# Fillers, early sums, highs, lows and the plan of an attention and expert kernel

## The chip, the cores and the metric

One core of one Trainium2 chip runs the whole program. The metric is the device time of one execution in microseconds; three executions of the kernel before took 981.32, 982.22 and 983.5 us, median 982.22.

## What is computed

The reference is an attention with a threshold, followed by four experts whose outputs are added with weights:

```python
scores = q @ k.T / sqrt(64)                    # q, k, v: 4 batches, 8 heads, 576 x 64
scores = where(scores >= max(scores) - tau, scores, -1e9)
attn = exp(scores - max(scores)); attn /= sum(attn)
x = (attn @ v)                                 # as 2304 rows of 512
p = domain_probs / sum(domain_probs)
for e in range(4):                             # w1: 512 x 1024, w2: 1024 x 512
    out += p[:, e:e + 1] * (relu(x @ w1[e]) @ w2[e])
```

## The kernel before, in words

**Numbers in two halves.** Everything is float32 in memory. Most products on PE are made from pairs of float16: a "high" is the value times a power of two, rounded to float16, and a "low" is what the rounding left; high x high, high x low and low x high are added in PSUM. The powers of two come from sums of squares: an engine squares a tensor and sums along the row (`squares`, L510), PE adds over partitions with a matrix of ones (`total`, L530), and five small DVE operations make the scale (`pow2`, L539). ACT or another engine then writes the high with that scale, and DVE the low with one operation on two inputs. The first batch's attention is done in float32 instead, and needs no highs and lows of q, k and v.

**Items and groups.** The attention is cut into 80 items (`item`, L1046): a pair of heads and a block of 128 queries, or the last 64 of each head. PE writes scores into tile S, which has one buffer of three banks (L1004, L1010); DVE takes them to SBUF with the maximum (L1066); GpSimd adds tau to the maximum (L1079); ACT takes the exponent (L1087); DVE masks and sums (L1096). In the first batch PE turns the result by matmuls into ET and ACT copies it to PT; later ACT and DVE make a high and a low (L1216, L1222) and DMA transposes bring them to PT. A group (`group`, L1254) multiplies PT with V (L1335) and writes X, the rows for the experts. The first batch takes one query block per pass: items 0 to 3 are block 0 of its four head pairs.

**Experts.** As soon as X of 128 or 256 rows is ready, the first two experts run on it (`unit`, L1427) between the items: L1454 makes the hidden layer, ACT does the ReLU with the factor wc (L1466) and the high (L1474), GpSimd the low (L1481), L1496 the second product. Sums go to DRAM as part. After the attention, the other two experts run with seven products in place of eight (`unit7`, L1635; L1690, L1770). A weight block of expert 0 or 1 is prepared in `w_prep` (L884): squares, total, pow2, then the high (L911, ACT) and the low (L936, DVE; for even blocks of expert 1 two GpSimd operations, L919 and L928, in its place). `w_done` (L944) makes wc and the other factors from the scales of all eight blocks. Expert 0's blocks are prepared in two fours, expert 1's in pairs. `w_pair` (L1533) does it for the last two experts; its squares on ACT (L523) wait for the load, and PE's total (L533) for the squares.

**What sets the order.** The class `Plan` (L23) holds every operation with its engine, an assumed time, what it reads and writes, and a priority. `schedule` (L130) plays the program through with these times and puts each engine's operations in one order, which is then emitted; on the chip each engine works through its order, and only semaphores hold it. The assumed times, the slack (`SLACK`, from time `SLACK0` on), the lateness of transposes (`LATE`) and `hold`, the earliest planned start of an item, change the order and nothing else. A mark `port` tells the plan that a DVE and a GpSimd operation hold each other up. Loads go through SP's queue.

**Fillers and early sums.** From 1.4 us of the plan on, where PE would be idle and has been busy less than 0.8 of the recent past, the plan sets a filler: four matmuls of 112 columns whose result nobody reads (`idle`, L1841; the trace has 228 matmuls, from 1.7 to 91.4 us). They go to columns 848 to 959 of tile S, which no score uses. The sums over partitions with a priority under 5 (`chain_tile`, L438: those of the first batch's v and of expert 0's two fours) go to columns 704 to 719 of S. The pool b, three PSUM banks, serves the first turns of q and k (tile TP, L705), until the experts' first product: then the same banks become the pool mm, and that product waits for all that read from b (`b_users`).

Of the kernel before, what the change touches and what calls it, by code (L numbers as in the profile page):

```python
# [14 lines left out]
ALU = mybir.AluOpType  # L15
# [7 lines left out]
class Plan:  # L23
# [18 lines left out]
    SLACK, SLACK0, LATE, seed = {}, 0, 0, 0  # L42
# [87 lines left out]
    def schedule(self):  # L130
# [21 lines left out]
        starts, self.plan, fills = [], {}, 0  # L152
# [22 lines left out]
        while True:  # L175
            progress = True
            while progress:
                progress = False
                for e in engines:
# [13 lines left out]
                    if pick is None:  # L193
                        if e == "PE" and self.fill and self.fill[0] <= now < self.fill[1] and (
# [9 lines left out]
                            self.ops.append(("PE", ns, self.fill[2], set(), (), 0.0, 0))  # L204
# [6 lines left out]
                    for u in use:  # L211
                        if u not in granted:
# [24 lines left out]
                    elif xfer:  # L237
# [64 lines left out]
def topk_attention_moe_kernel(  # L302
# [127 lines left out]
    n_am = 0  # L430
    for i in range(2):
        pl.pool(f"am{i}", 1)
        pl.kind(f"am{i}", f"am{i}", lambda _, i=i: s_all[:, 704 + 8 * i:712 + 8 * i])

    kind("AM", "ma", "ma", [128, 512], FP32)
    pl.loose.update(("AM", "TP", "ET0") + ())
# [11 lines left out]
    for name in ("TP", "ET0"):  # L448
        kind(name, "b", "b", [128, 512], FP32)
# [89 lines left out]
    def pow2(src, s_out, p_out, r, w, use, prio, tmp, au, add=None):  # L539
# [3 lines left out]
        def step(fn, rr, ww, more=()):  # L543
            dve(150, fn, rr, ww, use=use + list(more), prio=prio)
# [203 lines left out]
    def t_turn(g, prio):  # L748
# [28 lines left out]
        for x in range(2):  # L777
# [7 lines left out]
                prio=prio, xfer=-716,  # L785
# [33 lines left out]
    def v_prep(b, loaded, prio):  # L819
        st, V = ("st", ("v", b)), ("vr", b)  # L820
        vu, view, parts = loaded
        for i in range(NP):
# [3 lines left out]
                lambda: junk[:, 0:9 * D], parts, [("vm", b, i)], [vu[i], st], prio, i in (0, 1, 2, 3),  # L826
# [24 lines left out]
        for pr in range(NP) if b >= V32 else ():  # L851
# [4 lines left out]
                    out=pl.t(*u)[:, 0], in_=pl.t(*V)[:, pr], func=ACTF.Copy,  # L856
                    scale=v_c[:, b, 0:1],
                ),
                parts + [("vs", b)], [("vh", b, pr)], use=[V, u], prio=prio + 0.3 * pr,
# [24 lines left out]
    def w_prep(e, f0, nb, kd, prio, on_gp=lambda f: False):  # L884
# [98 lines left out]
    NI = len(items)  # L983

# [61 lines left out]
    def item(i):  # L1046
# [6 lines left out]
            ("rt", gi) if g // NP < V32 else ("ri", i),  # L1053
# [950 lines left out]
```

## Time and profile before

| what | value |
|---|---|
| median of three executions | 982.22 us |
| the profiled execution, its own time | 983.57 us |
| its span on the chip | 981.7 us |
| mean granted TensorE clock | 0.996 |
| PE matmuls busy | 953.0 us, 97%, x7796 |
| DVE busy | 733.6 us, 75%, x1826 |
| ACT busy | 556.5 us, 57%, x1181 |
| GpSimd (POOL) busy | 257.5 us, 26%, x400 |
| chain that ended last | PE 77%, DVE 8%, DMA 7%, ACT 4%, issue 2% |

Busy is the share of the span in which an instruction of that engine was under way; matmuls are pipelined, so a busy PE is not PE at its peak. The granted clock is the share of full speed that TensorE was given. The chain is followed back from the last instruction, at each step to what released it.

### The profile page before, as it was taken

How to read it: one execution, taken by the hardware profiler on the slowest of the kernel's cores; microseconds unless marked ns; L12 is line 12 of the kernel's file. 1: busy time of each engine (PE TensorE's matmuls, PEld its weight loads, DVE VectorE, ACT ScalarE, POOL GpSimd, SP SyncE). 2: the span in 40 equal slices, each digit the busy share in tenths (PEclk: the TensorE clock that was granted, in tenths of full speed). 3: DMA queues.
4: the chain of work that ended last, by engine and by line, in shares of the span. 5: the costliest groups of instructions: out<-in, count | busy, mean ns of one | idle time of the engine just before them, and what ended most of it. 6: DMA issues, size and time to landing. Idle time of an engine off the chain costs nothing.

```text
span 981.7 us, 20793 instructions
## 1 busy us (share of the span) xinstructions
PE 953.0 (97%) x7796; PEld 625.1 (64%) x7796; DVE 733.6 (75%) x1826; ACT 556.5 (57%) x1181; POOL 257.5 (26%) x400
## 2 busy tenths in 40 slices
PE   8799999999998999999999999999999999999998
PEld 6576655566655656566566756776666667666663
DVE  4799979999888988999763725897665588655551
ACT  5897877777777778786656758532222233212120
POOL 1155643354343344343332422200000010000000
PEclk9999999999999999999999999999999999999999
DMA  7812437778899679966662223301100102001001
GB/s 232 253 56 55 93 79 181 142 123 149 162 179 171 97 149 160 201 119 141 99 112 94 93 82 106 108 12 45 54 33 23 65 23 76 12 1 55 33 1 43
DMA packets 237397, 96.04 MB, mean 98 GB/s; under 512 B 201712, under 2 KB 224240, under 8 KB 237296
## 3 DMA queue, kind: packets, MB, share of 16 engines
q1 hardware_dynamic: 236208, 94.05, 43.1%
q8 instruction: 61, 1.00, 0.4%
q10 hardware_dynamic: 1088, 0.66, 0.2%
q14 instruction: 40, 0.33, 0.1%
HBM read 40.41 MB, written 14.16 MB: 56 GB/s over the span
## 4 chain that ended last, share of the span: by engine, by line
PE 77%; DVE 8%; DMA 7%; ACT 4%; issue 2%; SPq 1%; POOL 0%; DVEq 0%; ACTq 0%; POOLq 0%
PE mm L1770 19%; PE Q L1690 17%; PE mm L1496 16%; PE mm L1454 13%; PE S L1004 5%; PE av L1335 4%; DMA wraw<-in_moe_w_dram 3%; DVE E L1096 1%; DMA T<-R 1%; PE av L1344 1%; PE S L1010 1%; DVE SS L1066 1%; SPq L504 1%; DMA PT<-E 1%; ACT E L1087 1%
## 5 line engine op out<-in xcount | busy, mean ns | idle before, releaser
L1770 PE MATMUL mm<-WP,h 128*128 128x512 f16 x864 | 221.7, 379 | 0.0
L1496 PE MATMUL mm<-W,h 128*128 128x512 f16 x864 | 208.0, 381 | 0.1
L1454 PEld LDWEIGHTS <-W 128*128 128x128 f16 x2016 | 174.5, 98 | 31.4 <-issue 1.8
L1690 PEld LDWEIGHTS <-WP 128*128 128x128 f16 x1680 | 153.5, 98 | 63.5 <-issue 0.2
L1731 ACT ACTIVATE h<-qt 128x256 f16<-128x256 f32 (+1 forms) x160 | 62.1, 394 | 216.0 <-DVE qt L1710 215.6
L1454 PE MATMUL mm<-X,W 128*128 128x256 f16 (+1 forms) x1632 | 181.3, 267 | 0.0
L1710 DVE SCALAR_TENSOR_TENSOR qt<-Q,wc,qt 128x256 f32<-128x256 f32 (+1 forms) x280 | 124.2, 453 | 60.8 <-PE Q L1690 57.9
L1481 POOL TENSOR_TENSOR h<-hr,h 128x256 f16<-128x256 f32 (+1 forms) x168 | 130.1, 780 | 134.0 <-ACT h L1474 105.1
L1096 DVE SCALAR_TENSOR_TENSOR E<-SS,sm,E 128x576 f32<-128x576 f32 x144 | 123.7, 869 | 12.8 <-ACT E L1087 6.6
L1496 PEld LDWEIGHTS <-h 128*128 128x128 f16 x864 | 81.8, 99 | 77.9 <-issue 3.4
L1079 POOL TENSOR_SCALAR sm<-sm,tau_p 128x1 f32<-128x1 f32 x144 | 76.5, 532 | 184.1 <-DVE SS L1066 119.4
L1087 ACT ACTIVATE E<-SS,sm 128x576 f32<-128x576 f32 x144 | 109.1, 769 | 26.0 <-DVE SS L1066 17.6
L1770 PEld LDWEIGHTS <-h 128*128 128x128 f16 x864 | 82.9, 98 | 54.9
L1690 PE MATMUL Q<-T,WP 128*128 128x256 f16 (+1 forms) x960 | 117.8, 262 | 0.0
L1216 ACT ACTIVATE E<-E,ri 128x576 f16<-128x576 f32 (+1 forms) x120 | 83.1, 723 | 28.7 <-DVE ri L1194 11.4
L1222 DVE SCALAR_TENSOR_TENSOR E<-E,ri,E 128x576 f16<-128x576 f32 (+1 forms) x120 | 89.8, 779 | 8.6 <-ACT E L1216 8.0
L1066 DVE TENSOR_SCALAR_CACHE_REDUCE SS<-S,qc 128x576 f32<-128x576 f32 x108 | 85.7, 808 | 8.6 <-PE S L1010 3.4
L1466 ACT ACTIVATE hr<-mm,wc 128x256 f32<-128x256 f32 (+1 forms) x168 | 72.6, 435 | 33.4 <-PE mm L1454 30.5
L1690 PE MATMUL Q<-X,WP 128*128 128x256 f16 (+1 forms) x720 | 88.9, 262 | 0.0
L1647 POOL TENSOR_SCALAR psc<-pnv,wpm 128x2 f32<-128x2 f32 (+1 forms) x20 | 10.1, 505 | 287.2 <-DVE acc L1788 260.4
L1738 DVE SCALAR_TENSOR_TENSOR h<-qt,h 128x256 f16<-128x256 f32 (+1 forms) x160 | 61.4, 393 | 28.1 <-ACT h L1731 26.1
L1004 PE MATMUL S<-T 64*128 64x512 f16 (+3 forms) x440 | 71.8, 427 | 4.3 <-DVE SS L1066 4.0
(146 smaller groups left out, 1021.6 us busy)
## 6 DMA issues: line engine op xcount, KB each, us to landing
wraw<-in_moe_w_dram SPq DMA_DIRECT2D x64, 256.0 KB, 4.3
part<-acc SPq DMA_DIRECT2D x18, 256.0 KB, 2.6
X<-x_dram SPq DMA_DIRECT2D x9, 512.0 KB, 3.7
acc<-part SPq DMA_DIRECT2D x18, 256.0 KB, 3.9
out_dram<-acc SPq DMA_DIRECT2D x16, 256.0 KB, 2.3
x_dram<-X SPq DMA_DIRECT2D x7, 512.0 KB, 3.1
vr<-in_v_dram SPq DMA_DIRECT2D x12, 256.0 KB, 5.4
raw<-in_q_dram SPq DMA_DIRECT2D x24, 128.0 KB, 3.1
```

The source lines that it names most:

```text
L1004: nc.tensor.matmul(ps[:, 1024 * h:1024 * h + SM] if j < 4 else ps[rows(h), 0:SM], qm(h, a), km(h, c), start=(y == 0), stop=(y == last),)
L1066: nc.vector.tensor_scalar(out=pl.t(*ssu)[:, S * h:S * h + S], in0=pl.t(*su)[:, 960 * h:960 * h + S], scalar1=qc[:, g, 2:3] if g >= NP * T3 ...
L1087: lambda h=h: nc.scalar.activation(out=pl.t(*eu)[:, S * h:S * h + S], in_=pl.t(*ssu)[:, S * h:S * h + S], func=ACTF.Exp, scale=-1.0, bias= ...
L1096: lambda h=h, col=col: nc.vector.scalar_tensor_tensor(out=pl.t(*eu)[:, S * h:S * h + S], in0=pl.t(*ssu)[:, S * h:S * h + S], scalar=pl.t(* ...
L1216: nc.scalar.activation(out=o, in_=e, func=ACTF.Copy, scale=pl.t(*ru)[:, h:h + 1])
L1222: nc.vector.scalar_tensor_tensor(out=o, in0=e, scalar=pl.t(*ru)[:, h:h + 1], in1=hh, op0=ALU.mult, op1=ALU.subtract,)
L1454: nc.tensor.matmul(ps[:, 0:n], w[:, wp, 0, c * 128:(c + 1) * 128], x[:, c, xp, c0:c0 + n], start=(i == 0), stop=(i == len(seq) - 1),)
L1481: lambda hu=hu, hru=hru: nc.gpsimd.tensor_tensor(out=pl.t(*hu)[:, 1, 0:n], in0=pl.t(*hru)[:, 0:n], in1=pl.t(*hu)[:, 0, 0:n], op=ALU.subtra ...
L1496: nc.tensor.matmul(ps, h[:, hp, 128 * i:128 * i + 128], w[:, wp, 1, :], start=(f == f0 and hp == 0 and wp == 0), stop=(f == f1 - 1 and hp ...
L1690: nc.tensor.matmul(reg(r), w[:, wp, o:o + 128], xb(b, c, xp), start=(n == 0), stop=(n == 5),)
L1710: lambda: nc.vector.scalar_tensor_tensor(out=tmp(o), in0=reg(r), scalar=wcs, in1=tmp(i), op0=ALU.mult, op1=ALU.add),
L1770: nc.tensor.matmul(ps, ht()[:, hp, 128 * i:128 * i + 128], w[:, wp, o:o + 512], start=(f == 0 and hp == 0 and wp == 0), stop=(f == NF - 1 ...
```

## The change

The fillers get a tile of their own kind in pool b, are set only while the plan has a free bank there, and end where the first bank goes to mm. The early sums get the kind AMB in the same pool, and their readers join `b_users`. The highs of expert 0's eight blocks go from ACT to GpSimd. The four blocks of expert 1 that had their lows on GpSimd have them on DVE. The squares of v, four per batch, go from DVE to ACT. The rest is in the plan: item i is held to -40 + 6.7 i us in place of 6 i; slack of 100 ns is added on DVE and ACT beside 700 on PE, all from 10 us on and not from 60; transposes count as 1.5 us late and not 1.2, other loads as 1.5 us late; the small steps of `pow2` count as 205 ns, sums of weights as 488; the priority of the first batch's v goes from 1.5 to 2.5; the assumed times are drawn with a spread of 3%; two GpSimd operations get the port mark. Groups under 12, and not batches under 1, are called float32; that is the same set.

```diff
-    SLACK, SLACK0, LATE, seed = {}, 0, 0, 0
+    SLACK, SLACK0, LATE, LATL, seed = {}, 0, 0, 0, 0
...
-                        if e == "PE" and self.fill and self.fill[0] <= now < self.fill[1] and (
+                        if e == "PE" and self.fill and filling and spare["b"] and self.fill[0] <= now < self.fill[1] and (
...
-                            self.ops.append(("PE", ns, self.fill[2], set(), (), 0.0, 0))
+                            u = ("ID", fills)
+                            self.slot[u], self.users["b", u] = spare["b"].pop(0), 1
+                            heapq.heappush(events, (free[e] + 160 + self.FREED, 3, ("b", u)))
+                            self.ops.append((
+                                "PE", ns, lambda u=u: self.fill[2](self.tiles[u]), set(), (u,), 0.0, 0
+                            ))
...
+                        filling = filling and self.kinds[u[0]][0] != "mm"
...
                             end = max(end, free[e] + 1900) + self.LATE
+                        elif now >= self.SLACK0:
+                            end += self.LATL
...
-    pl.SLACK = {"PE": 700, "DVE": 0, "ACT": 0,
+    pl.SLACK = {"PE": 700, "DVE": 100, "ACT": 100,
                 "s": 0, "b": 0, "ma": 0, "mm": 0, "q": 0}
-    pl.LATE = 1200
-    pl.SLACK0 = 60000
-    pl.seed = 0
+    pl.LATE, pl.LATL = 1500, 1500
+    pl.SLACK0 = 10000
+    pl.seed = 2
...
     def chain_tile(key, prio):
-        nonlocal n_am
         if prio >= 5:
             return ("AM", key)
-        n_am += 1
-        return (f"am{n_am % 2}", key)
+        return ("AMB", key)
...
-    for name in ("TP", "ET0"):
+    for name in ("TP", "ET0", "ID", "AMB"):
...
-            dve(150, fn, rr, ww, use=use + list(more), prio=prio)
+            o = dve(205, fn, rr, ww, use=use + list(more), prio=prio)
+            if more and more[0][0] == "AMB":
+                b_users.append(o)
...
-                lambda: junk[:, 0:9 * D], parts, [("vm", b, i)], [vu[i], st], prio, i in (0, 1, 2, 3),
+                lambda: junk[:, 0:9 * D], parts, [("vm", b, i)], [vu[i], st], prio, i in (),
...
-            act(
+            if (e, f) in tuple((0,f) for f in range(8)):
+                gp(
+                    1116,
+                    lambda u=u, W=W, f=f: nc.gpsimd.tensor_scalar(
+                        out=pl.t(*W)[:, 0], in0=pl.t(*u), scalar1=wsc[:, e, f:f + 1],
+                        scalar2=1.0, op0=ALU.mult, op1=ALU.mult,
+                    ),
+                    rr, [("wh", e, f)], use=[u, W], prio=prio(f),
+                )
+            else:
+              act(
                 1142,
...
+    P32 = 12
...
-        pl.hold[o] = (0,6.0)[0] + 1000 * (0,6.0)[1] * i
+        pl.hold[o] = (-40000,6.7)[0] + 1000 * (-40000,6.7)[1] * i
...
-            [("pnv", b) for b in bs] + [("wpm2", u)], [("sc", u, name)], use=[sc], prio=top,
+            [("pnv", b) for b in bs] + [("wpm2", u)], [("sc", u, name)], use=[sc], prio=top, port=1,
...
             dve(
-                424,
+                488,
...
-        def idle():
+        def idle(t):
             for _ in range(4):
-                nc.tensor.matmul(s_all[:, 848:960], ident16, ident16[:, 0:112], start=True, stop=True)
+                nc.tensor.matmul(t[:, 0:112], ident16, ident16[:, 0:112], start=True, stop=True)
...
-        GP0 = lambda f: False
-        GP1 = lambda f: f % 2 == 0
+        GP0 = lambda f: f in ()
+        GP1 = lambda f: f in ()
...
-        at(0, v_prep, 0, v_load(0, -36), 1.5)
+        at(0, v_prep, 0, v_load(0, -36), 2.5)
```

## Rows read from the trace of the kernel before

**Rows 1.** Busy time by stretch: length, engines' busy us (instructions), clock, DMA share, GB/s.

```profile
20.00:60.00 40.00, 32.26 (x377) 23.92 (x377) 33.36 (x105) 33.64 (x63) 7.25 (x16) 1.00 0.70 200
...
60.00:105.00 45.00, 42.62 (x458) 30.49 (x456) 43.62 (x120) 38.71 (x93) 30.14 (x39) 1.00 0.19 54
...
160.00:520.00 360.00, 351.43 (x3072) 222.35 (x3070) 314.06 (x799) 265.10 (x542) 151.45 (x232) 1.00 0.78 146
...
640.00:982.00 342.00, 337.73 (x2419) 222.28 (x2417) 217.39 (x499) 83.48 (x199) 9.49 (x18) 1.00 0.10 33
```

**Rows 2.** Timeline, DVE, before 60 us: start, us, instruction, idle before and its releaser.

```profile
26.22 0.16 DVE L547 TENSOR_SCALAR_CACHE_REDUCE st<-S 128x4 f32<-128x4 f32 x1 [0.76 <-PE S L1843]
...
31.32 0.82 DVE L1066 TENSOR_SCALAR_CACHE_REDUCE SS<-S,qs 128x576 f32<-128x576 f32 x1 [0.92 <-PE S L1843]
...
34.64 0.16 DVE L552 TENSOR_SCALAR st<-S 128x4 f32<-128x4 f32 x1 [2.21 <-PE S L1010]
...
50.40 0.16 DVE L552 TENSOR_SCALAR st<-S 128x4 f32<-128x4 f32 x1 [0.62 <-PE S L1843]
```

**Rows 3.** Groups by line and shape: count, busy us, mean ns, idle before.

```profile
L1096 DVE SCALAR_TENSOR_TENSOR E<-SS,sm,E 128x576 f32<-128x576 f32 x144 | 123.7, 869 | 12.8 <-ACT E L1087 6.6 <-POOL sm L1079 4.0 <-POOL h L1481 1.6
...
L911 ACT ACTIVATE W<-wraw,wsc 128x1024 f16<-128x1024 f32 x16 | 17.8, 1146 | 4.6 <-DVE wpow L566 2.4 <-DVE wsc L562 2.2
...
L523 ACT ACTIVATE junk<-raw 128x512 f16<-128x512 f32 x24 | 15.0, 626 | 2.2 <-DVE junk L514 1.9
...
L514 DVE SCALAR_TENSOR_TENSOR junk<-vr 128x576 f16<-128x576 f32 x12 | 10.1, 840 | 0.0
...
L523 ACT ACTIVATION_READ_ACCUMULATOR junk<-raw 128x1 f32 x24 | 4.6, 191 | 0.0
...
L514 DVE SCALAR_TENSOR_TENSOR junk<-V 128x576 f16<-128x576 f32 x4 | 3.0, 755 | 0.0
```

**Rows 4.** Busy time by stretch, around the two falls of the clock.

```profile
308.00:312.00 4.00, 4.00 (x37) 2.74 (x32) 2.02 (x9) 1.57 (x4) 0.27 (x1) 0.57 1.27 156
...
570.00:576.00 6.00, 6.00 (x22) 2.50 (x23) 5.35 (x17) 3.62 (x7) 1.30 (x2) 0.72 0.00 0
```

**Rows 5.** Timeline of the waits ahead of them, PE and ACT.

```profile
306.34 0.30 PE L1335 MATMUL av<-PT,V 128*64 128x256 f16 x2 [1.67 <-DMA PT<-E]
...
568.68 1.06 ACT L523 ACTIVATE WP<-wraw 128x1024 f16<-128x1024 f32 x1 [3.22 <-DMA wraw<-in_moe_w_dram]
...
569.88 0.38 PE L533 MATMUL QA<-st,ones 128*128 128x2 f32 x2 [2.25 <-ACT WP L523]
```

**Rows 6.** GpSimd's conversion L919 by itself: shortest, median and longest ns.

```profile
L919 POOL TENSOR_SCALAR wraw<-wraw,wsc x4: 1116/1288/1772, 68.5 to 100.8; 128x1024 f32<-128x1024 f32 x4
```

**Rows 7.** Timeline, expert 1's preparation: GpSimd, DVE and PE, 70 to 106 us.

```profile
70.32 2.12 POOL L928 TENSOR_TENSOR W<-wraw,W 128x1024 f16<-128x1024 f32 x1
...
70.38 3.15 DVE L936 SCALAR_TENSOR_TENSOR W<-wraw,wsc,W 128x1024 f16<-128x1024 f32 x1
...
80.79 1.98 DVE L562 TENSOR_SCALAR wsc<-st 128x2 int32<-128x2 int32 x1
...
84.54 0.33 PE L1146 MATMUL ET<-ident,E 128*128 128x128 f32 x1 [2.13 <-ACT PT L1026]
...
86.80 2.38 DVE L936 SCALAR_TENSOR_TENSOR W<-wraw,wsc,W 128x1024 f16<-128x1024 f32 x1 [0.28 <-ACT W L911]
...
105.13 2.68 DVE L1096 SCALAR_TENSOR_TENSOR E<-SS,sm,E 128x576 f32<-128x576 f32 x1
```

**Rows 8.** Timeline, second four of expert 0: lows, first fillers, wc.

```profile
54.91 4.88 DVE L936 SCALAR_TENSOR_TENSOR W<-wraw,wsc,W 128x1024 f16<-128x1024 f32 x4
...
56.18 1.15 PE L1843 MATMUL S<-ident 128*128 128x112 f16 x20
...
59.71 0.16 DVE L968 TENSOR_TENSOR wc<-qf 128x8 f32<-128x8 f32 x1
```

**Rows 9.** Tile S, the score matmuls: ns, first and last start in us.

```profile
L1004 PE MATMUL S<-T x440: 372/376/693, 9.9 to 502.7; 64*128 64x512 f16 x96, 64*64 64x512 f16 x24, 64*128 64x512 f32 x23, 64*64 64x512 f32 x4
```

More of the change, by code (lines that the diff above doesn't have):

```diff
@@ L151, in schedule @@
                 heapq.heappush(ready[o[0]], (o[5], i))
-        starts, self.plan, fills = [], {}, 0
+        starts, self.plan, fills, filling = [], {}, 0, True
         bus, until, moved = {"DVE": (-1, -1e9), "POOL": (-1, -1e9)}, {}, []
@@ L429, in topk_attention_moe_kernel @@
     pl.kind("S", "s", lambda _: s_all)
[L430 to L433, printed above, removed]
     kind("AM", "ma", "ma", [128, 512], FP32)
-    pl.loose.update(("AM", "TP", "ET0") + ())
+    pl.loose.update(("AM", "TP", "ET0", "AMB") + ())
     def chain_tile(key, prio):
-        nonlocal n_am
         if prio >= 5:
             return ("AM", key)
-        n_am += 1
-        return (f"am{n_am % 2}", key)
+        return ("AMB", key)
     first_s = ExitStack()
@@ L850, in v_prep @@
         gp(600, go, ["pn", ("vp", b)], [("pnv", b)], prio=prio)
-        for pr in range(NP) if b >= V32 else ():
+        if b < V32 and P32 == 12:
+            return
+        prio += 8 if b < V32 else 0
+        for pr in range(NP):
             u = ("V", (b, pr))
@@ L855, in v_prep @@
                 lambda pr=pr, u=u: nc.scalar.activation(
-                    out=pl.t(*u)[:, 0], in_=pl.t(*V)[:, pr], func=ACTF.Copy,
-                    scale=v_c[:, b, 0:1],
+                    out=pl.t(*u)[:, 0], in_=view(pr), func=ACTF.Copy, scale=v_c[:, b, 0:1],
                 ),
-                parts + [("vs", b)], [("vh", b, pr)], use=[V, u], prio=prio + 0.3 * pr,
+                parts + [("vs", b)], [("vh", b, pr)], use=[vu[pr], u], prio=prio + 0.3 * pr,
             )
@@ L863, in v_prep @@
                 lambda pr=pr, u=u: nc.vector.scalar_tensor_tensor(
-                    out=pl.t(*u)[:, 1], in0=pl.t(*V)[:, pr], scalar=v_c[:, b, 0:1],
+                    out=pl.t(*u)[:, 1], in0=view(pr), scalar=v_c[:, b, 0:1],
                     in1=pl.t(*u)[:, 0], op0=ALU.mult, op1=ALU.subtract,
                 ),
-                parts + [("vs", b), ("vh", b, pr)], [("vl", b, pr)], use=[V, u],
+                parts + [("vs", b), ("vh", b, pr)], [("vl", b, pr)], use=[vu[pr], u],
                 prio=prio + 0.3 * pr, port=1,
@@ L1052, in item @@
             ("T16" if g >= NP * T32 else "T", g), ("S", i), ("SS", i), ("E", i), ("sm", i),
-            ("rt", gi) if g // NP < V32 else ("ri", i),
-            ("PT32" if g // NP < V32 else "PT", gi),
+            ("rt", gi) if gi < P32 else ("ri", i),
+            ("PT32" if gi < P32 else "PT", gi),
         )
-        one = g // NP < V32
+        one = gi < P32
         heads = range(2) if j < 4 else range(1)
@@ L1179, in turn @@
             lambda: nc.sync.dma_start(out=dst(), in_=src(), transpose=True), r, w,
-            use=use, prio=i + 0.2, xfer=-0.62 * nbytes,
+            use=use, prio=i + 0.2 - 0, xfer=-0.62 * nbytes,
         )
@@ L1261, in group @@
         ru, bu, au, xu, pu, V = (
-            ("rt", gi), ("rb", gi), ("av", gi), ("x32", gi), ("PT32" if b < V32 else "PT", gi),
-            ("V32" if b < V32 else "V", (b, pr)),
+            ("rt", gi), ("rb", gi), ("av", gi), ("x32", gi), ("PT32" if gi < P32 else "PT", gi),
+            ("V32" if gi < P32 else "V", (b, pr)),
         )
         r16 = ("r16", gi)
-        one = b < V32
+        one = gi < P32
         def rec():
@@ L1328, in av_ @@
             vv, av, t = pl.t(*V), pl.t(*au), pl.t(*pu)
-            pairs = ((0, 0),) if b < V32 else ((0, 0), (0, 1), (1, 0))
+            pairs = ((0, 0),) if one else ((0, 0), (0, 1), (1, 0))
             ts = lambda r, tp, c, c0, c1: t[r, c, tp, c0:c1] if one else t[r, tp, c, c0:c1]
-            va = (lambda r, vp, x: vv[r, x, :]) if b < V32 else (lambda r, vp, x: vv[r, vp, x, :])
+            va = (lambda r, vp, x: vv[r, x, :]) if one else (lambda r, vp, x: vv[r, vp, x, :])
             for c in range(4):
@@ L1342, in av_ @@
                     r = slice(64 * h, 64 * h + 64)
-                    k = n if b < V32 or not h else nm
+                    k = n if one or not h else nm
                     nc.tensor.matmul(
@@ L1651, in unit7 @@
                 [("pnv", b) for b in bs] + [("wpm2", u)], [("sc", u, name, j)], use=[sc[j]],
-                prio=top,
+                prio=top, port=1,
             )
@@ L1901, in topk_attention_moe_kernel @@
         assert not todo
-        gone = {"ma", "s", "am0", "am1", "tl", "tt", "vr", "v", "ss", "e", "pt", "rb", "x32", "rt", "r16", "sm"}
+        gone = {"ma", "s", "tl", "tt", "vr", "v", "ss", "e", "pt", "rb", "x32", "rt", "r16", "sm"}
         ends = {i for i, o in enumerate(pl.ops) if any(pl.kinds[x[0]][0] in gone for x in o[4])}
```

8 lines of the change are left out of this document (4 added, 4 removed).

## Prediction

> **What bounds the kernel now.** I read the busy time by stretches first [rows 1]. From 640 us to the end PE is busy 337.7 of 342 us, and in 160 to 520 us 351.4 of 360. PE's work does not change, so the whole time is that work plus what PE loses, and most of the loss lies ahead of 60 us: in 20 to 60 us PE is busy 32.3 of 40, part of that in fillers, while DVE and ACT are each busy 33.4 and 33.6 of 40. Neither is full; they wait for each other along the chain scores, exponent, turn, product. In 60 to 105 us it is another picture: DVE is busy 43.6 of 45 us, so what DVE does there is the path. A microsecond won before 105 us is kept only if PE is full afterwards, which the later stretches of [rows 1] say it nearly is.
>
> Next I looked in the timeline for what DVE waits for before 60 us. Four of its waits end on tile S without needing S's scores [rows 2]: the maximum's read waits 0.92 us for a filler; the readers of the early sums wait 0.76, 2.21 and 0.62 us for fillers or for the scores written after the sum. That is 4.5 us. Fillers and early sums lie in unused columns of the score tile, and are ordered against it all the same.
>
> Then the price of each edited operation [rows 3], and last the two places where the clock fell [rows 4, 5]: granted clock 0.57 over 308 to 312 us and 0.72 over 570 to 576, after PE had waited 1.67 us for a transposed PT, and 2.25 us for the sum of squares of a weight that ACT could not begin because its load was late (ACT waited 3.22 us). Between 1.2 and 2.4 GHz the loss is 4 x 0.43 = 1.7 us and 6 x 0.28 = 1.7 us, on top of the waits.
>
> **The change, part by part**, against the profiled execution, 983.57 us; it stands 1.35 us above the median of the runs, 982.22.
>
> *Fillers and early sums off tile S.* Removes the 4.5 us of DVE waits [rows 2]. They stand on a chain that also waits for ACT, so not all of it shows. Adds: a filler or a sum needs one of the three banks of the first turns, and waits for the copy out of it; those copies end before the second filler stretch, so I cost this at nothing, with the finished turns as the cover. If turns came later, a filler would wait with PE behind it. Ends: 0 and -4.5. I take **-3**.
>
> *First expert's highs from ACT to GpSimd, first squares of v from DVE to ACT.* ACT loses 8 x 1.146 = 9.2 us and gains four squares; the nearest row is a 512-wide square, 0.626, so 0.70 at 576 elements plus 0.19 for reading the sum: 3.6 us. Net -5.6 us on ACT; DVE loses 4 x 0.755 = 3.0 us [rows 3]. GpSimd gains eight conversions. The trace has no float16 high on GpSimd; the nearest row is L919, the same size to float32: 1.12 to 1.77 us [rows 6], so 9 to 14 us of an engine that is busy 7.3 of 40 us there [rows 1]. What is queued behind each high on GpSimd is the threshold L1079 of a running item, for which DVE's masking L1096 waits. And GpSimd and DVE hold each other up, as the rows of the second expert show: a DVE operation started beside GpSimd's subtraction ran to that one's end ([rows 7], 1.98 us for an operation on two elements, where the small L968 takes 0.16 [rows 8]). If every high and every low exclude each other, a block of four takes 4 x (1.12 + 1.22) = 9.4 us instead of the 4.9 us of its lows [rows 8]: 4.5 us longer, 9 us for both blocks. Ends: -5.6 (ACT's relief, no exclusion) and +9. Halfway is +1.7, and DVE's 3.0 us speak for less: I take **0**.
>
> The Trainium skill has this as a rule, in SBUF — State Buffer, section SBUF: two separate sides: DVE and GpSimd share one pair of ports as a lock, and whichever instruction starts first keeps it to its end, while the other stands. The trace agrees for the subtractions [rows 7]. By that rule alone the sum would take the +9 end, and the total would be 9 us longer; that is the third rival below.
>
> *What the highs free.* The factors wc, which the first expert's ReLU needs, stand on DVE behind four lows in a row, 4.88 us, and end at 59.9 us; PE fills its time with fillers from 56.18 on, 40 matmuls in three stretches, by the first one's 1.15 us for 20 some 2.3 us [rows 8]. With a high of over 1.1 us ahead of each low, the order of the plan can set wc in between. Ends: 0 (wc stays behind the lows) and -3 (fillers and 0.7 us beside them). I take **-2**.
>
> *Second expert's lows to DVE.* Removes four pairs on GpSimd, and what they cost DVE: L936 took 3.15 and 2.38 us instead of 1.22, L562 1.98 instead of 0.16, L1096 2.68 instead of its mean of 0.87 [rows 3, 7, 8]: 1.93 + 1.16 + 1.82 + 1.81 = 6.7 us. Adds four lows, 4 x 1.22 = 4.9 us. DVE is full there, so -1.8 us is on the path; in the middle of it PE stood 2.13 us [rows 7], of which I count half. GpSimd's thresholds and h lows no longer queue behind 2.1 us subtractions. Ends: -6.7 (the new lows in gaps) and +4.9 (the old stalls beside the path). I take **-3**.
>
> *Squares of v of the later batches.* DVE loses 12 x 0.840 = 10.1 us, ACT gains 12 x 0.89 = 10.7 us [rows 3]. In 160 to 520 us ACT is busy 265 of 360 and DVE 314 [rows 1], so ACT can take it; but PE has only 8.6 us to win there. If ACT's room is gone, each square delays an exponent by 0.9 us. Ends: -4 and +3. I take **-1**.
>
> *Slack for loads and waits.* It is only in the plan: instructions stay, their order moves. A load counted 1.5 us later sets the sum of squares behind more matmuls: the wait of 2.25 us [rows 5] would shrink to about 0.75, and the clock then may hold. Ends: 0 and -3.9; I take -2.5. The transposes get only 0.3 us more against a wait of 1.67, so there I take -0.5 (ends 0 and -4.5). Together **-3**. 700 ns for PE from 10 us on makes the plan see longer gaps and set more fillers; they use time that PE has, as long as the gaps are real.
>
> *Even pace, drawn durations, 100 ns on DVE and ACT.* The last scores start at 502.7 us [rows 9]; the hold for item 79 moves from 474.0 to 6.7 x 79 - 40 = 489.3 us, both earlier than that, so the hold is hidden under DVE's work; a gap in PE shows if DVE gets ahead by over 13 us. All the rest is another order of the same work: I take **0**, with two stalls like that near 570 us either way, 2 x (2.25 + 1.7) = 8 us. Changed costs in the plan (205, 488 ns), port marks and the names that go by group 12 emit nothing and cost nothing.
>
> Sum: -3 + 0 - 2 - 3 - 1 - 3 + 0 = **-12 us**: 971.6 for an execution like the profiled one, 970.2 for the median. I predict **970 us**.
>
> **The rivals.** (1) *No change, 982 us.* The front part only moves: items 0 to 3 end sooner, but 60 to 105 us is DVE's, 43.6 of 45 us busy, and what PE gains in front it waits there. For it: that stretch. Against: DVE loses work there too. (2) *More, 959 us.* The favourable ends together: -4.5, -4, -3, -4.5, -2, -5 = -23, which asks that both falls of the clock go. For it: each is tied to one late transfer. Against: the transposes get just 0.3 us. (3) *Slower, 988 us: the lock.* Eight highs on GpSimd meet eight lows and the small operations of the sums on DVE in the first 60 us. Both blocks take 9.4 us, +9; the gain of wc goes, +2; and the thresholds behind the highs hold up DVE, one high each, 8 x 1.12 = 9 us at most, of which I take 7: 970 + 18 = 988. It decides once highs and thresholds cost DVE over 12 us there. For it: the rows of the second expert [rows 7]. Against: GpSimd's conversion has one input and short rows beside other DVE work (L919's shortest is 1.12 us), and most of DVE's work in that stretch is not lows.
>
> On the clock the Trainium skill, TensorE: Matmul & The Clock Gate, section Part 1, says that the array falls to half clock when it has not been busy enough. The trace has it [rows 4]. Since fillers now stop at the first expert's matmul, one new fall after that point would by this rule add 1.7 us to the sum.
>
> **Numbers.** Forecast 0.52, no change 0.13, more 0.15, slower 0.20. So faster by over 0.2% 0.67, within 0.2% 0.13, slower 0.20; 0.2%, some 2 us, is about what a measurement of this kernel can tell from no change. The range: the forecast's own unknown order is +-8 us (962 to 978); rival 2 lies at 959 and rival 3 at 988, so 957 to 989 leaves out about 2 in 10, the far ends of both.
>
> **What would show it.** Right: no DVE wait ended by a filler, none on the early sums; the first expert's matmuls start some 5 us before 54 us and its ReLU does not wait for wc; L936 at 1.2 to 1.3 us in the second expert; PE in 20 to 60 us with fewer fillers; no wait over 1 us and clock 1.00 at the passage near 570 us. Wrong: GpSimd's highs at 2 us and more, with L1079 and L1096 late behind them; the first expert's matmuls later than 54 us; new falls of the clock in 105 to 520 us; a last score before 489 us with PE idle.

## The result: 972.76 us, 9 us less, won in part in other places than forecast

The changed kernel took **972.76 us** (median of four executions, 972.27 to 975.21); the kernel before took 981.77 beside it (four, 979.63 to 983.50). The ratio is 0.9919, 95% interval 0.9896 to 0.9942; the medians differ by 9.0 us. The forecast was 970 in 957 to 989. The profiled execution took 972.27 us, its span was 970.5.

The busy time by stretch of the changed kernel, columns as in [rows 1], the last stretch cut to the shorter span:

```profile
20.00:60.00 40.00, 31.42 (x369) 23.36 (x367) 35.05 (x100) 28.16 (x66) 19.31 (x24) 1.00 0.75 221
60.00:105.00 45.00, 43.76 (x408) 29.19 (x405) 42.09 (x116) 38.71 (x93) 21.93 (x34) 0.96 0.19 48
160.00:520.00 360.00, 353.82 (x3084) 224.71 (x3081) 306.85 (x774) 273.88 (x560) 150.86 (x234) 1.00 0.75 143
640.00:969.00 329.00, 326.19 (x2332) 213.81 (x2329) 211.13 (x487) 82.72 (x194) 6.10 (x18) 1.00 0.11 36
```

The engines' shares went the way the change moves the work: in 20 to 60 us ACT fell from 33.6 to 28.2, GpSimd rose from 7.3 to 19.3; in 160 to 520 us DVE fell from 314 to 307 and ACT rose from 265 to 274. PE in 20 to 60 us is *less* busy than before (31.4 against 32.3), while it runs fewer fillers: 128 matmuls against 152 in this stretch, 152 against 228 in all.

To see where the time came from I lined the two traces up by TensorE's own work: the matmul records summed by their size, fillers left out, and for each amount of work the time at which it had begun. The table is good to about 1 us, its row of 400 us only to some 3: summed by plain columns that row's gain is 5 to 7 us.

| own work begun | before, us | after, us | won so far |
|---|---|---|---|
| 20 us | 46.1 | 37.0 | 9.0 |
| 25 us | 54.0 | 51.7 | 2.2 |
| 30 us | 63.3 | 62.5 | 0.8 |
| 45 us | 81.2 | 80.8 | 0.4 |
| 60 us | 104.1 | 100.2 | 3.9 |
| 200 us | 261.6 | 258.3 | 3.3 |
| 400 us | 488.9 | 480.3 | 8.6 |
| 480 us | 576.1 | 564.5 | 11.6 |
| 860 us | 965.7 | 954.2 | 11.5 |

Nine microseconds are won by 37 us and all but 0.8 are given back by 62 us. One microsecond stands in all rows from the start: in this execution PE's first turns begin at 4.7 us and take 2.8, in the one before they begin at 5.0 and take 3.5, and the traces of the runs below lie on both sides. So the front keeps nothing that can be told from that. More comes later: 3 us at the second expert (81 to 104 us), 5 between there and 560 us, 3 at the passage near 570 us. (These two executions differ by 11.3 us, the medians by 9.0.)

The front gain, and its loss. Timeline of DVE and GpSimd in the changed kernel, columns as in [rows 2]; then the eight highs (L917) and all sixteen lows (L951) by themselves, shortest, median and longest ns:

```profile
27.68 0.16 DVE L550 TENSOR_SCALAR_CACHE_REDUCE st<-AMB 128x4 f32<-128x4 f32 x1
...
33.03 0.15 DVE L555 TENSOR_SCALAR st<-AMB 128x4 f32<-128x4 f32 x1
...
34.88 0.81 DVE L1082 TENSOR_SCALAR_CACHE_REDUCE SS<-S,qs 128x576 f32<-128x576 f32 x1
...
36.35 5.82 DVE L951 SCALAR_TENSOR_TENSOR W<-wraw,wsc,W 128x1024 f16<-128x1024 f32 x3
...
42.35 1.27 DVE L951 SCALAR_TENSOR_TENSOR W<-wraw,wsc,W 128x1024 f16<-128x1024 f32 x1
...
48.04 0.77 DVE L610 TENSOR_SCALAR rs<-rs 128x18 f32<-128x18 f32 x1
...
58.84 0.17 DVE L983 TENSOR_TENSOR wc<-qf 128x8 f32<-128x8 f32 x1
```

```profile
34.77 6.33 POOL L917 TENSOR_SCALAR W<-wraw,wsc 128x1024 f16<-128x1024 f32 x4 [1.79 <-DVE r L1296]
...
47.16 2.71 POOL L917 TENSOR_SCALAR W<-wraw,wsc 128x1024 f16<-128x1024 f32 x2 [4.62 <-ACT PT L1042]
```

```profile
L917 POOL TENSOR_SCALAR W<-wraw,wsc x8: 1112/1120/2082, 34.8 to 53.8; 128x1024 f16<-128x1024 f32 x8
...
L951 DVE SCALAR_TENSOR_TENSOR W<-wraw,wsc,W x16: 1269/1284/2134, 36.4 to 100.3; 128x1024 f16<-128x1024 f32 x16
```

The early sums (L550, L555, which answer to the waiting rows of [rows 2]) wait for nothing now. But the four highs (L917) and four lows (L951) of the first block take from 34.77 to 43.62 us: 8.85 us, where the worst price of the forecast was 9.4. Two highs run at 1.12 us beside DVE's maximum reads of S (L1082, 0.81 as ever). Then highs and lows take turns: three lows take 5.82 us where 3 x 1.28 = 3.84 would do, and a high up to 2.08. The small operation at 48.04 us takes 0.77; beside highs on ACT (the first experiment) the same one takes 0.18. The Trainium skill's rule of SBUF — State Buffer, section SBUF: two separate sides, which names among DVE's operations those with two inputs in SBUF and those in a two-port mode, agrees: the lows have two such inputs and exclude the highs, the reads of S do not. The factors wc (L983) end at 59.0 us, hardly before the 59.9 of [rows 8], and PE waits for what follows:

```profile
44.62 1.40 PE L1133 MATMUL ET<-ident,E 128*128 128x128 f32 x8 [1.62 <-DVE E L1112]
...
51.47 0.66 PE L1133 MATMUL ET<-ident,E 128*128 128x128 f32 x4 [2.20 <-DVE x L1382]
...
59.83 0.83 PE L1470 MATMUL mm<-X,W 128*128 128x128 f16 x12 [3.06 <-ACT hr L1482]
```

In the second expert the picture is as forecast: the eight lows on DVE, the four moved ones among them, take 1.27 to 1.42 us (two shown) where [rows 7] had 3.15 and 2.38.

```profile
66.75 1.28 DVE L951 SCALAR_TENSOR_TENSOR W<-wraw,wsc,W 128x1024 f16<-128x1024 f32 x1 [1.17 <-ACT W L926]
...
87.76 1.28 DVE L951 SCALAR_TENSOR_TENSOR W<-wraw,wsc,W 128x1024 f16<-128x1024 f32 x1
```

The clock, by stretches: the two falls of [rows 4] are not in this execution, and there is a new one behind the 3.06 us wait, 0.57 over 61 to 65 us:

```profile
61.00:65.00 4.00, 4.00 (x28) 2.79 (x25) 3.93 (x15) 1.85 (x6) 2.94 (x4) 0.57 0.02 6
...
308.00:312.00 4.00, 2.83 (x37) 1.81 (x34) 3.39 (x13) 3.90 (x12) 0.53 (x2) 1.00 0.66 122
570.00:576.00 6.00, 6.00 (x104) 5.94 (x103) 0.69 (x6) 5.80 (x19) 1.67 (x4) 1.00 0.13 44
```

At the upper level 4 us would have held 4 x 0.43 = 1.7 us more. The Trainium skill, TensorE: Matmul & The Clock Gate, section Part 1, says that the array drops to half clock when it was not kept busy enough; this row and those of [rows 4, 5] agree, each fall standing behind a wait of PE. Not every wait brings one: those of 1.62 and 2.20 us shown above are followed by none in this execution.

### The profile page after: what moved, and what is told of

Read it like the earlier page. It is cut to its first block, busy times and chain, and to the rows that moved or that the text cites. A ratio compares the mean times of both kernels' runs of the same rounds, so it can differ in the third digit from the quotient of the medians.

```text
span 970.5 us, 20653 instructions
## 1 busy us (share of the span) xinstructions
PE 945.8 (97%) x7720; PEld 620.4 (64%) x7720; DVE 721.8 (74%) x1798; ACT 558.8 (58%) x1205; POOL 249.1 (26%) x400
## 4 chain that ended last, share of the span: by engine, by line
PE 76%; ACT 7%; DMA 6%; DVE 5%; issue 3%; POOL 1%; SPq 1%; ACTq 0%; DVEq 0%; POOLq 0%
PE mm L1786 19%; PE Q L1706 16%; PE mm L1470 14%; PE mm L1512 13%; PE S L1020 5%; PE av L1351 4%; DMA PT<-E 2%; DMA wraw<-in_moe_w_dram 2%; PE S L1026 1%; ACT E L1103 1%; ACT junk L524 1%; PE av L1360 1%; SPq L505 1%; PE ET L1133 1%; DVE E L1112 1%
## 5 line engine op out<-in xcount | busy, mean ns | idle before, releaser
L1786 PE MATMUL mm<-WP,h 128*128 128x512 f16 x864 | 219.4, 379 | 0.0
L1512 PE MATMUL mm<-W,h 128*128 128x512 f16 x864 | 205.1, 379 | 1.1 <-ACT hr L1482 1.1
L1112 DVE SCALAR_TENSOR_TENSOR E<-SS,sm,E 128x576 f32<-128x576 f32 x144 | 120.1, 845 | 22.5 <-ACT E L1103 14.5
L1095 POOL TENSOR_SCALAR sm<-sm,tau_p 128x1 f32<-128x1 f32 x144 | 73.2, 509 | 182.3 <-DVE SS L1082 125.9
L1082 DVE TENSOR_SCALAR_CACHE_REDUCE SS<-S,qc 128x576 f32<-128x576 f32 x108 | 85.7, 809 | 15.8 <-PE S L1026 9.5
L1663 POOL TENSOR_SCALAR psc<-pnv,wpm 128x2 f32<-128x2 f32 (+1 forms) x20 | 6.7, 337 | 290.2 <-DVE acc L1804 253.2
```

The source lines that it names most:

```text
L1082: nc.vector.tensor_scalar(out=pl.t(*ssu)[:, S * h:S * h + S], in0=pl.t(*su)[:, 960 * h:960 * h + S], scalar1=qc[:, g, 2:3] if g >= NP * T3 ...
L1112: lambda h=h, col=col: nc.vector.scalar_tensor_tensor(out=pl.t(*eu)[:, S * h:S * h + S], in0=pl.t(*ssu)[:, S * h:S * h + S], scalar=pl.t(* ...
L1512: nc.tensor.matmul(ps, h[:, hp, 128 * i:128 * i + 128], w[:, wp, 1, :], start=(f == f0 and hp == 0 and wp == 0), stop=(f == f1 - 1 and hp ...
L1786: nc.tensor.matmul(ps, ht()[:, hp, 128 * i:128 * i + 128], w[:, wp, o:o + 512], start=(f == 0 and hp == 0 and wp == 0), stop=(f == NF - 1 ...
```

## The experiments

Each is the changed kernel with one thing altered. In the first three, the eighth and the ninth to eleventh the plan's order stays as it is and only the instruction written out (or its tile) differs, so they undo an engine move without another order. They ran in three rounds on two chips (runs 1 to 4 and 9 to 12 on one, 5 to 8 on the other), in which the kernel before took 980.13, 980.33 and 980.67 us. The ratio is the record's estimate against the kernel before of the same round, not the quotient of the two medians. The changed kernel itself, run again in the second round (four executions), took 973.38 us (971.30 to 975.12), 0.9931 (0.9909 to 0.9954); "over after" below is the difference of medians against that.

| run | median (range, count) | ratio, 95% | over after |
|---|---|---|---|
| highs on ACT | 975.28 (973.61 to 980.01, 10) | 0.9950 (0.9928 to 0.9971) | +1.9 |
| fillers and sums on S | 977.30 (974.33 to 979.82, 10) | 0.9966 (0.9944 to 0.9988) | +3.9 |
| second expert's lows on GpSimd | 974.87 (973.68 to 979.39, 10) | 0.9948 (0.9927 to 0.9970) | +1.5 |
| wc first | 973.28 (971.53 to 976.62, 10) | 0.9930 (0.9908 to 0.9952) | -0.1 |
| old plan | 975.64 (974.12 to 976.88, 6) | 0.9949 (0.9928 to 0.9970) | +2.3 |
| loads on time | 977.44 (975.38 to 978.83, 10) | 0.9974 (0.9964 to 0.9985) | +4.1 |
| all squares of v on DVE | 979.18 (974.51 to 980.91, 10) | 0.9982 (0.9964 to 1.0000) | +5.8 |
| first batch's squares on DVE | 972.74 (971.21 to 974.66, 4) | 0.9904 (0.9875 to 0.9933) | -0.6 |
| later squares on DVE | 979.22 (974.11 to 983.81, 10) | 0.9980 (0.9952 to 1.0007) | +5.8 |
| no fillers | 973.79 (971.12 to 976.87, 5) | 0.9925 (0.9899 to 0.9951) | +0.4 |
| seed 0 | 978.61 (976.85 to 979.49, 10) | 0.9970 (0.9955 to 0.9986) | +5.2 |

Only loads on time, all squares of v and seed 0 have intervals clear of the changed kernel's 0.9909 to 0.9954. By the ratios some differences come out smaller than by the medians, by up to 2 us: 3.4 for fillers and sums on S, 4.8 for the later squares, 3.8 for seed 0, -2.6 for the first batch's squares.

The single undoings add up to far more than 9 us: they are not shares of a sum. An undoing in a fixed order shows what one piece costs in an order planned without it; what the move itself won against the kernel before can be less.

**1. Highs of the first expert on ACT.**

```diff
-                    lambda u=u, W=W, f=f: nc.gpsimd.tensor_scalar(
-                        out=pl.t(*W)[:, 0], in0=pl.t(*u), scalar1=wsc[:, e, f:f + 1],
-                        scalar2=1.0, op0=ALU.mult, op1=ALU.mult,
+                    lambda u=u, W=W, f=f: nc.scalar.activation(
+                        out=pl.t(*W)[:, 0], in_=pl.t(*u), func=ACTF.Copy, scale=wsc[:, e, f:f + 1],
                     ),
```

> The kernel after, with the first expert's eight highs issued on ACT again, each at its place in the unchanged order. Theory (the lock eats the front part's gain): the first block of highs and lows, 34.8 to 43.6 us in the kernel after, takes 3 us less, the first expert's matmuls start at 50 to 52 us and not at 54.6, total 968 to 970 us. Rival (ACT's relief pays for the lock): ACT has 9.2 us more to do before 58 us, the first expert's matmuls start at 55 to 59 us, total 974 to 978.

Measured 975.28 us, +1.9; the first expert's matmuls start at 59.2 us. So the rival's outcome, not clear of noise. Its first high on ACT, two of the DVE lows and one of the PE waits:

```profile
36.63 1.15 ACT L917 ACTIVATE W<-wraw,wsc 128x1024 f16<-128x1024 f32 x1
...
37.81 1.28 DVE L950 SCALAR_TENSOR_TENSOR W<-wraw,wsc,W 128x1024 f16<-128x1024 f32 x1 [0.52 <-ACT W L917]
...
43.55 1.27 DVE L950 SCALAR_TENSOR_TENSOR W<-wraw,wsc,W 128x1024 f16<-128x1024 f32 x1
...
50.61 0.18 DVE L610 TENSOR_SCALAR rs<-rs 128x18 f32<-128x18 f32 x1
...
53.10 0.66 PE L1132 MATMUL ET<-ident,E 128*128 128x128 f32 x4 [1.91 <-ACT rb L1334]
```

Without the lock the block takes 8.2 us from the first high to the end of the last low (36.63 to 44.82) in place of 8.85: 0.7 us less and not 3. It begins 1.9 us later, 0.9 of which this trace is late from its first matmuls on, and PE waits for ACT instead. Moving the highs to GpSimd is a small gain net, by the medians some 2 us. By own work this trace is level with the changed kernel's at 64 us, but for those 0.9 us, so the gain is not won in the front.

**2. Fillers and early sums back on tile S.**

```diff
-    for name in ("TP", "ET0", "ID", "AMB"):
+    for name in ("TP", "ET0"):
         kind(name, "b", "b", [128, 512], FP32)
+    pl.kind("ID", "b", lambda i: s_all)
+    pl.kind("AMB", "b", lambda i: s_all[:, 704 + 8 * i:712 + 8 * i])
...
-                nc.tensor.matmul(t[:, 0:112], ident16, ident16[:, 0:112], start=True, stop=True)
+                nc.tensor.matmul(s_all[:, 848:960], ident16, ident16[:, 0:112], start=True, stop=True)
```

> The kernel after, with fillers and early sums written to the unused columns of the score tile S again, the order unchanged. Theory (freeing S is worth some 3 us): DVE waits of 0.6 to 2.2 us for fillers and for the early sums come back before 55 us, total 974 to 977 us. Rival (what S frees is lost again behind the highs): the waits come back, the first expert's matmuls start within 1 us of 54.6, total 972 to 973.

Measured 977.30 us, +3.9. DVE's waits for S are back, among them one for a filler (L1861) and one of an early sum's reader for the scores written after it:

```profile
29.31 0.16 DVE L552 TENSOR_SCALAR_CACHE_REDUCE st<-S 128x4 f32<-128x4 f32 x1 [0.45 <-PE S L1861]
...
37.24 0.16 DVE L557 TENSOR_SCALAR st<-S 128x4 f32<-128x4 f32 x1 [1.35 <-PE S L1028]
```

By TensorE's own work this run is 5 us behind the changed kernel's at 42 us and stays so to the end; 1 us of it stands from the first matmuls on. So freeing S is worth about 4 us in this order, though the front as a whole kept 0.8 us at 62 us. What takes it back there no run singles out: without the lock (run 1) nothing is won by 64 us, and with wc earlier (run 4) a lead of 2.6 us is gone by 100.

**3. Second expert's lows as two GpSimd operations.** For blocks 0, 2, 4 and 6 of expert 1, as in the kernel before:

```diff
...
+                if e == 1 and f % 2 == 0:
+                    nc.gpsimd.tensor_scalar(
+                        out=pl.t(*u), in0=pl.t(*u), scalar1=wsc[:, e, f:f + 1], scalar2=1.0,
+                        op0=ALU.mult, op1=ALU.mult,
+                    )
+                    nc.gpsimd.tensor_tensor(
+                        out=pl.t(*W)[:, 1], in0=pl.t(*u), in1=pl.t(*W)[:, 0], op=ALU.subtract
+                    )
+                    return
...
```

> The kernel after, with the lows of the second expert's even blocks issued as two GpSimd operations again, at their places in the unchanged order. Theory (the lows on DVE are worth some 3 us): DVE operations of 2 us and more beside GpSimd's subtraction come back between 65 and 105 us, total 975 to 978 us. Rival (DVE's gaps take them): total 972 to 973.

Measured 974.87 us, +1.5. The other lows are held up again:

```profile
91.15 2.26 POOL L955 TENSOR_TENSOR W<-wraw,W 128x1024 f16<-128x1024 f32 x1
...
91.34 3.16 DVE L959 SCALAR_TENSOR_TENSOR W<-wraw,wsc,W 128x1024 f16<-128x1024 f32 x1
```

The mechanism is as I had it; its worth by the medians is half of my 3 us, just under the theory's range, and not clear of noise. The profiled execution, 979.39 us, is the slowest of the ten, so it shows the stretching and not the price.

**4. wc ahead of two of the lows.**

```diff
-        at(1, w_done, 0, range(0, NF, 4), EP(NF - 1))
+        at(1, w_done, 0, range(0, NF, 4), 1.5)
```

> The kernel after, with the priority of the first expert's factors wc raised from 4.4 to 1.5, so that they stand behind two lows of the second block and not behind four; some operations around it change places too. Theory (wc late is what PE waits for at 59.8 us, and the fall of the clock follows from it): PE's wait of 3.06 us for ACT's ReLU is gone, the clock stays 1.00 over 61 to 65 us, total 967.5 to 970 us. Rival (DVE, full until 105 us, is the path there): the wait goes, PE waits elsewhere before 105 us, total 972 to 973.

Measured 973.28 us, -0.1. wc comes 4.1 us earlier and the 3.06 us wait is gone:

```profile
54.73 0.15 DVE L983 TENSOR_TENSOR wc<-qf 128x8 f32<-128x8 f32 x1
...
56.91 2.17 PE L1470 MATMUL mm<-X,W 128*128 128x128 f16 x36
```

By own work it leads by 2.6 us at 66 us, by 1.6 at 87, and by nothing at 100 us. The clock, 1.00 over 61 to 65 us, fell at 52, 86 and 179 us in this profile. Ten executions give the same median, so the lead is worth nothing in the end: the first rival's outcome, for this part.

**5. Changed kernel again**, for the spread.

> The kernel after itself, as the measure for the runs beside it and for those before. Both theories: 970 to 974 us, 6 to 10 us under the kernel before on the same chip; in other executions the clock may fall in other places than near 61 us.

Measured 973.38 us; the clock fell at 48 and at 62 us here, at 61 alone in the first profile. A single profile does not say where every execution's clock falls.

**6. The old plan with all moved operations**: no slack for DVE and ACT, PE's slack from 60 us on, transposes 1.2 us late, other loads on time, seed 0, hold of 6 i.

```diff
-    pl.SLACK = {"PE": 700, "DVE": 100, "ACT": 100,
+    pl.SLACK = {"PE": 700, "DVE": 0, "ACT": 0,
...
-    pl.LATE, pl.LATL = 1500, 1500
-    pl.SLACK0 = 10000
-    pl.seed = 2
+    pl.LATE, pl.LATL = 1200, 0
+    pl.SLACK0 = 60000
+    pl.seed = 0
...
-        pl.hold[o] = (-40000,6.7)[0] + 1000 * (-40000,6.7)[1] * i
+        pl.hold[o] = (0,6.0)[0] + 1000 * (0,6.0)[1] * i
```

> The kernel after with the plan's parameters of before (transposes 1.2 us late, other loads not late, slack on PE alone and from 60 us on, no drawn durations, items held at 6 i us): the moved operations and banks alone. Theory (of the 11 us by which the PE work of the profiled execution came earlier, 3 to 4 stood before 105 us and 7 to 8 came from the plan): total 976 to 980 us, with a wait of 1 to 3 us near 565 us for a late weight load. Rival (the moves also relieve DVE in the attention): total 971 to 974.

Measured 975.64 us, +2.3 over after and 4.7 under the kernel before (interval of the ratio 0.9928 to 0.9970, so 3 to 7 us), between the theory and the rival: with these numbers of the old plan the moved work carries about two thirds. The changed costs of `pow2` and of the sums, the port marks and v's priority stay in this run.

**7. Loads on time**: `LATL` 0, all else as changed.

```diff
-    pl.LATE, pl.LATL = 1500, 1500
+    pl.LATE, pl.LATL = 1500, 0
```

> The kernel after with ordinary loads counted as on time (LATL 0 in place of 1500), transposes still 1.5 us late. Theory (the slack for loads took away the wait near 565 us): the wait of 2 us for the sum of squares of a late weight is back, with a fall of the clock behind it, total 974 to 977 us. Rival (that wait went by the order's chance): no such wait, total 971 to 974.

Measured 977.44 us, +4.1, but not where I had put it. PE in the first 50 us and at the passage of [rows 5]:

```profile
45.00 0.66 PE L1133 MATMUL ET<-ident,E 128*128 128x128 f32 x4 [3.34 <-DVE E L1112]
...
570.45 0.38 PE L534 MATMUL QA<-st,ones 128*128 128x2 f32 x2 [0.60 <-ACT WP L524]
```

The load there is still 2.91 us late for ACT, PE loses 0.60 us, and the clock over 570 to 576 us is 1.00. The old plan's run has no PE wait there at all, with loads on time and a load 0.87 us late. So the slack is not what cleared that passage; which order the plan falls into is. The 4 us lie in waits elsewhere, as that of 3.34 us at 45 us, and in falls of the clock at 46, 90 and 305 us.

**8. All squares of v on DVE.** The argument makes `squares` write the DVE form under an ACT entry of the plan.

```diff
...
-                lambda: junk[:, 0:9 * D], parts, [("vm", b, i)], [vu[i], st], prio, i in (),
+                lambda: junk[:, 0:9 * D], parts, [("vm", b, i)], [vu[i], st], prio, i in (), True,
```

> The kernel after with the sixteen squares of v issued on DVE again, at their places in the unchanged order. Theory (they are worth little, some 1 us, since PE is full in the attention): total 972 to 975 us. Rival (DVE is the attention's bound): DVE has 12 us more to do before 320 us, total 978 to 984.

Measured 979.18 us, +5.8 (5.0 by the ratios): the largest effect of an engine move, from the part I had priced at -1 and 0. So I split it.

**9. The first batch's four alone** (`b < 1` for `True`).

> Changed kernel, but the squares of v of the first batch alone (4) are written for DVE again, everything else and the order as it is. All 16 together cost 5.8 us over the changed kernel. Theory A (the first batch's 3.0 us of DVE lie on the path before the first scores, and the ACT gain of 3.6 us does not pay): 2 to 3.5 us over the changed kernel by the ratio to the kernel before, 975.5 to 977 us. Rival B (ACT is as full as DVE there, the two cancel, as the prediction had it with 0 net for ACT and DVE): within 1 us of the changed kernel, 972.5 to 974.5.

Measured 972.74 us, -0.6. Its busy time in the front:

```profile
20.00:60.00 40.00, 30.83 (x365) 22.95 (x364) 37.27 (x108) 25.94 (x58) 19.99 (x24) 1.00 0.74 214
```

DVE has 2.2 us more there, ACT 2.2 less, and the time is the same: rival B, and the zero of the prediction.

**10. The twelve of the later batches alone** (`b >= 1`).

> Changed kernel, but the 12 squares of v of the later batches are written for DVE again, everything else and the order as it is. Theory A (DVE, 307 of 360 us busy in 160 to 520 us, is what PE's gaps there hang on, and 10.1 us more on it fall where the plan has DVE work back to back): 3 to 6 us over the changed kernel, 976.5 to 979.5, lost in steps at the batches' squares after 100 us, with the mean granted clock at 0.995 or lower. Rival B (my term of -1): 0 to 1.5 us over, 973 to 975.

Measured 979.22 us, +5.8: all of it. The PE waits of its trace, with the squares (L524) that stand on DVE just ahead of the first, and the busy time of the attention's stretch:

```profile
104.66 0.76 DVE L524 SCALAR_TENSOR_TENSOR junk<-vr 128x576 f16<-128x576 f32 x1
...
106.08 0.75 DVE L524 SCALAR_TENSOR_TENSOR junk<-vr 128x576 f16<-128x576 f32 x1
...
106.76 0.55 DVE L1385 SCALAR_TENSOR_TENSOR x<-av,v_c,rb 128x320 f32<-128x320 f32 x1
...
107.36 0.66 PE L1136 MATMUL ET<-ident,E 128*128 128x128 f32 x4 [2.03 <-DVE x L1385]
...
186.29 0.82 PE L1023 MATMUL S<-T 64*128 64x512 f16 x6 [2.42 <-DVE SS L1085]
...
308.46 0.82 PE L1023 MATMUL S<-T 64*128 64x512 f16 x6 [2.08 <-DVE SS L1085]
```

```profile
160.00:520.00 360.00, 350.52 (x3072) 223.69 (x3072) 310.02 (x786) 267.54 (x543) 154.65 (x235) 1.00 0.76 142
```

At the same places the changed kernel has no wait at 108 us, 0.65 (for ACT) at 187.89 and 1.17 at 310.58. PE is busy 350.5 of 360 us, less than the 351.4 of the kernel before. What PE waited for in 160 to 520 us (total us, times, longest), in the kernel before, the changed kernel and this run:

```profile
PE av L1335 <- DMA PT<-E: 4.1, 4, 1.7
PE S L1004 <- DVE SS L1066: 4.0, 4, 1.6
...
PE S L1020 <- DVE SS L1082: 3.3, 6, 1.2
PE av L1351 <- DMA PT<-E: 1.8, 2, 1.3
...
PE S L1023 <- DVE SS L1085: 7.2, 7, 2.4
```

So the squares cost 3.9 us of waits for DVE when they are put back into the order planned without them. Against the kernel before, though, whose order was planned with them on DVE, the waits for DVE fell only from 4.0 to 3.3 us, and those for transposes from 4.1 to 1.8. The 5.8 us are therefore not shown to be what the move won; a plan made anew with these squares on DVE was not run. ACT, too, waited 6.9 us for the squares on DVE in this run, since both write the same scratch tile; the waits of PE name DVE.

This profiled execution (974.11 us) is the run's fastest. The other nine took 975.2 to 983.8, with mean clocks of 0.990 to 0.996 against this one's 0.998, so about 5 us of the 5.8 are in executions that have no profile; that they are falls of the clock behind such waits fits, but was not looked at one by one.

**11. No fillers.**

```diff
         def idle(t):
-            for _ in range(4):
-                nc.tensor.matmul(t[:, 0:112], ident16, ident16[:, 0:112], start=True, stop=True)
+            return
```

> Changed kernel in which the fillers emit nothing (152 matmuls on the unit matrix less, which no output uses), order as it is. Theory A (the fillers hold the clock at its upper level in the first 60 us): granted clock near 0.5 in stretches between 25 and 55 us, where TensorE's real work of some 25 us then takes longer: +3 to +8 us, 976 to 981. Rival B (they only take places of PE, as the waits of DVE for them in the kernel before suggest, and the clock falls at 48 and 61 us come with them too): within 1.5 us of the changed kernel.

Measured 973.79 us, +0.4: nothing. The clock does fall:

```profile
45.00:53.00 8.00, 5.64 (x42) 4.41 (x42) 7.83 (x25) 4.49 (x10) 4.98 (x4) 0.75 0.42 112
```

but DVE is busy 7.83 of these 8 us and PE only 5.64: the changed kernel's PE is busy 5.72 there at clock 1.00. As I read it, slow matmuls fill time that PE would have waited. Fillers bought nothing here that five executions can show; what they cost before was DVE's waits for them.

**12. No draw of durations.** Seed 0 is not another draw: the spread of 3% is applied only when the seed is not 0, so the plan's times are the plain ones, as in run 6.

```diff
-    pl.seed = 2
+    pl.seed = 0
```

> Changed kernel with another draw of the planned durations (seed 0 in place of 2), all instructions the same, another order. Theory A (the drawn order is worth nothing certain, as my term of 0 with +-8 has it): within 4 us of the changed kernel either way, 970 to 977.5, with stalls in other places. Rival B (the draw was picked and is a good part of the 7 to 9 us): over 4 us slower, 978 to 982, like loads on time (977.4).

Measured 978.61 us, +5.2. It shows among others as

```profile
46.63 1.61 PE L1133 MATMUL ET<-ident,E 128*128 128x128 f32 x8 [2.56 <-DVE E L1112]
...
61.95 2.08 PE L1020 MATMUL S<-T 64*128 64x512 f32 x4 [4.03 <-DVE SS L1082]
```

The same instructions in another order lose 5 us by the medians and 3.8 by the ratios: rival B by the medians, at its border by the ratios, and within the ±8 that the prediction gave the order. Under this plan about half of the gain or more rests on the drawn order of seed 2; the old plan, which has no draw either, loses only 2.3. How far one draw differs from another was not run.

No run is clearly faster than the changed kernel.

## Why the prediction was right, and where it was not

The total was right (-12 forecast, -9.0 measured, inside the range), in part by luck: some terms hold, others were wrong and partly made up for each other, and the order, put at 0, carries between a third (run 6) and two thirds (run 12) of the gain.

- *Fillers and early sums off S, -3*: right. No DVE wait is ended by a filler, none stands on the early sums, and putting them back costs 3 to 4 us. What I expected to see beside it was wrong: the first expert's matmuls begin at 54.6 us, not 5 us before 54.
- *First expert's highs and first squares, 0*: right as a sum, within noise (1.9 us for the highs). The lock, which I took by half, is there between highs and lows, and the first block takes 8.85 us. Its price is not the 4.5 us a block that I had as the worst: with the highs on ACT the block still takes 8.2 in this order. The first squares are worth nothing that can be measured. Rival 3 had the mechanism, but not its price: the first experiment, without the lock, has PE waiting for ACT in its place.
- *wc earlier, -2*: wrong. The step that failed is "the order of the plan can set wc in between": it can, as run 4 shows, but at wc's priority of 4.4 it did not, and wc stands behind the fourth low and ends at 59.0 us. And even at 54.9 us it would have given nothing (-0.1), its lead being gone by 100 us.
- *Second expert's lows, -3*: mechanism right; 1.5 us by the medians, not clear of noise.
- *Squares of v of the later batches, -1*: open in size. Put back into the order planned without them they cost 5 to 6 us, beyond my end of -4. "PE has only 8.6 us to win there" did not say what PE waited for: 4.0 us of it were DVE, 4.1 late transposes. DVE, busy 314 of 360, was no spare engine: 9 us of work back on it cost waits of 2.0 to 2.4 us at three places, though ACT does each square more slowly (0.68 + 0.19 us against 0.75 + 0.08). Between the two kernels, though, the waits for DVE fell by just 0.7 us, which is near my -1.
- *Slack for loads, -3*: size near by luck (4.1 with loads on time), mechanism wrong. I priced it from two events of one execution, and the wait at the passage went in other ways too. The runs show that the slack sets the whole order.
- *Even pace and draw, 0 with ±8*: right as a bound; without the draw the kernel loses 3.8 to 5.2 us, which the 0 left out.
- *Rival 1* is right for the front: of 9 us won by 37 us, 0.8 are left at 62 us. Rival 2 was added up from smaller ends than those of the parts, whose sum is -32 and not -23; it was not reached either way.
- Of the new fall of the clock, which I had named as a 1.7 us risk: it came, at 61 to 65 us.

## What to carry to other kernels

Where an engine that feeds TensorE is 87% busy over hundreds of microseconds, work put back on it can show up as waits of TensorE (here 9 us of squares cost 5 to 6 us), so such work is worth trying on another engine, even one that does it more slowly. But an undoing in a fixed order is not the price of the move: compare the waits of both kernels as well. A gain at the front must be followed to the next stretch that another engine owns; there it can vanish whole. A planned order has a scatter of its own (here 4 to 5 us between a drawn and an undrawn plan), so an edit of a few microseconds is tested with the order held fixed, and two events in one profiled execution are no price.

## What was unexpected of the hardware

- DVE's lows and GpSimd's single-input conversions excluded each other: lows took up to 2.13 us in place of 1.28, conversions up to 2.08 in place of 1.12, while DVE's maximum reads of S beside the conversions kept their 0.81. An 18-element operation on DVE rose from 0.18 to 0.77 us beside a conversion, and GpSimd's pnv (128x16) took 1.31 us beside a low.
- The kernel before, 72 times on two chips, took 975.2 to 985.5 us, and its time goes with its mean granted clock: nine executions at 1.000 have a mean of 978.0 us, thirteen at 0.991 to 0.994 one of 982.8. So the falls at 308 and 571 us of the profiled one are not in every execution.
- A lower clock need not cost time: without fillers the mean clock was 0.988 to 0.995, against 0.996 to 0.998 with them, at medians of 973.79 and 973.38. Among the five without fillers the lowest clock, 0.988, still goes with the longest time, 976.87.
